# Linear attention and a phase mixer on one core: two batches' k and v in runs of nine tokens, their product in quarters of the array, and a new order of issue

## The chip, the cores and the metric

The kernel runs on one core of one Trainium2 chip. The metric is the device time of one execution in microseconds (us), as the median over several executions.

The engines are TensorE (PE, with its weight loads as PEld), VectorE (DVE), ScalarE (ACT), GpSimd (POOL) and SyncE (SP). Each works through its own queue of instructions in order; they wait for each other through semaphores. Transfers are issued from the queues of SP, ACT and POOL. Those that change the type on the way (fp32 in memory, fp16 on chip) are issued by POOL.

## The reference

Eight batches, eight heads, 576 tokens, head width 64. First a linear attention without softmax, normalised per head, then a mixer over tokens with a phase that comes from the data.

```python
kv  = einsum('bhsd,bhse->bhde', k, v)
out = einsum('bhsd,bhde->bhse', q, kv)
x   = out / sqrt(mean(out * out, -1) + 1e-6) * g_norm      # then (8, 576, 512)
theta = x @ w_theta
y = w_tok_r @ (x * cos(theta)) + w_tok_i @ (x * sin(theta))    # over tokens
u = x + y
result = u + relu(u @ w_ch)
```

## The kernel before

The kernel is a list of small tasks. Each has an engine and a function that issues its instructions. `TURNS`, a list of task numbers written out by hand, gives the one order in which the tasks are issued, and so the order of each engine's queue; a letter behind a number says which engine takes a task that several could do (A for ACT, D for DVE), and `r16` or `r4` stands for that many matmuls on constants, which keep TensorE busy while it has nothing else.

A batch's 576 tokens are four tiles of 128 (j = 0 to 3) and a tail of 64 (j = 4), whose eight heads are packed in halves on 128 partitions. Per batch:

- `load k`, `load v`, `load q`: fp32 k and v through SP, two buffers each (`NKV`); q through POOL as fp16, three buffers.
- `kv`: the product of k and v for each pair of heads (`kv_piece`), and `ko`: its copies into a block diagonal tile `kbd` (`kv_out`).
- `qt` and `qo`: q is turned by TensorE against the identity and copied from PSUM, in batches below `QD`; from batch `QD` on a DMA transpose does it, issued by SP (`qd`, `q_turn_dma`).
- `raw`: turned q times `kbd`. `sq`, `ss`, `rt`, `x`: squares (ACT), their sums (DVE), the power -1/2 (POOL), and the scaled x (DVE), which reads `raw` in PSUM.
- `xt` and `xo`: x turned and copied. `th`: the matmul with `w_theta`. `pt`, `ar`, `ab`, `si`, `co`: reduction of the angle, sine and cosine. `z`: x times both. `zv`: the tail's z, moved by four small transfers issued by POOL.
- `y`: the mix over tokens, for two halves of the columns (y0, y1) and four groups of channels, each in three thirds of three matmuls; the last third needs all z and the moved tail. `um`: u.
- `ut`, `uo`, `v`, `fin`, `st`: u turned back, its matmul with `w_ch`, the sum with relu, the store.

Once, at the beginning, the two token matrices are turned (`wt`, copied by `wo`), and `w_ch` is scaled (`wc`). SP's queue holds back batch 1's k and v until the imaginary token matrix has landed (`hold s`). PSUM has two banks for turned tiles, two for `raw` and four for everything else (`acc`); batch 0's `raw` tiles are in those four as well.

The layout of k and v in SBUF matters here. From batch 1 on, a partition holds four tokens in a row of each head (1024 bytes), and a second transfer brings the last 64 tokens to 64 partitions of a fifth slice (256 bytes each), whose other 64 partitions hold zeros (`pad`). The product then takes five matmuls over 128 rows for each head. In batch 0 a head's 576 tokens lie as nine tokens on each of 64 partitions (2304 bytes in one run), two heads of a pair above each other on 128 partitions:

```python
    def pairs_in(eng, dst, src, b, lo, hi):
        eng.dma_start(
            out=nines(dst)[:, lo:hi, :],
            in_=src[b].rearrange("h (p j) d -> (h p) (j d)", j=NN).rearrange(
                "(n r) x -> r n x", r=P)[:, lo:hi, :],
        )
```

and the product takes nine matmuls over 64 rows for each head, even heads in one quarter of the array, odd heads in the opposite quarter. SP loads k of batch 0 in two transfers, ACT loads v in two.

Of the kernel before, what the change touches and what calls it, by code (L numbers as in the profile page):

```python
# [29 lines left out]
0 2 8 1 4 9 3 5 6 7 11 12 13 r16 29 14 30 15 37 44 45A 38A 32 31D 33 39 46 40 51 34 41 52 47 42 35D  # L30
48 36A 58 65 53 66 54 59 49 67 10 43 55 60 61 68 56 50 62 69 70 16 r4 129 57 125 17 130 63 126 72 18
73D 121 19 71 81 122A 74 20 22 82D 64 21 108 133 109D 198 99 134A 83 199 100D 200 90 75 84 91D 85
127 101 137 76 86 128D 87 92 88 93 102 77 138 131 123 110 132D 94 89 78 111 79 96 205 95 103 112 80
113 206 207 97 114 124 98 115 208 116 159 210A 209D 160 211 212D 232 139 119 118 120 117 140 233D
213 225 214 104 226D 135 155 215 227 228 105 106 216 163 156 218 164 136D 28D 229 230 219D 217 231
220 221 255 234 222 23 24 201 197 26A 107 223 202 157 161 256 246 141 224 158 162 239 165 257 203
240 235 142 247D 204 357 248 166 236 258 249 143 241 259 358 237 260 250 167 168 151 152 147 144 148
145 242 252 353 388 366 514 377 251 238 243 244 25 146 264 265D 245 149 169 273 261 253 262 170 274D
266 153 282 150 154 27D 267 283 275 181 284 276 360 254 268 285 361 286 362 363 191 287 182 288 269
277 289 270 290 263 364D 278 293 291 292 359 294 271 192 365 186 183 188 389 184 187 390 185 279 525  # L40
# [3 lines left out]
403 404D 322 436 384 437 175 502 503 504 304 305 396 385 438 306 397 342 405 386 343 398 327 400 406  # L44
376 399 508 509 347 510 387 407 408 401 328 348 511 193 409 421 329 412 344 512 410 413 194 422 513D
# [5 lines left out]
579D 675 561 447 544 448 449 558 676 667 559 450 574 545 575 495 580 581 582 546 490 668 562 492 455  # L51
# [5 lines left out]
599 604 605 600 707 730 614 718D 731 601 816 619 620 732 817 733 606 826 709D 602 818 734 695 719  # L57
720 847 827 621 615 848 828 697 721 622 722 628 616 617 710 723 711 698 829 618 735 736 819 849 712
713 820 952 724 850 714 851 830 737 738 629 715 953 954 955 643 833 625 630 623 956 834 957 624 644
759 739 716 725 831 835 836 626 740 741 760 838 865 959 839 837 866D 852 631 499 627 945 632 500  # L60
# [5 lines left out]
1097D 873 1098 788 995 996 789 985 778 899 1100 986 900 1111 887 776 647 1121 1101 987D 1102 1112  # L66
777 1103 779 901 888 1022 895 889 780 785 790 896 1004 890 902 1113 1104 988 897 989 990 898 1114
903 904 905 997 891 991 906 1005D 1115 1023 992 998 892 791 1024 893 993 792 1025 999 1000 894 1026
# [753 lines left out]
```

## Time and profile before

| | |
|---|---|
| median of 3 runs | 225.78 us (225.51 to 227.9) |
| profiled execution: time, span | 224.09 us, 222.3 us |
| busy: PE, PEld | 202.9 us (91%), 143.2 us (64%) |
| busy: DVE, ACT, POOL | 175.2 us (79%), 131.6 us (59%), 103.4 us (47%) |
| mean granted clock of TensorE | 0.977 |
| transfers | 40.88 MB, mean 184 GB/s |

How to read it: the span runs from the first to the last instruction of the profiled execution; its time includes what lies around that. A row of a timeline or a chain begins with start and length in us. A row of a group ends in busy time, mean length of one, and idle time before it with the releaser behind an arrow. A matmul's length covers its way through the array, so matmuls in a row overlap, and the time that each adds is the stretch divided by their number. A row of transfer issues has their number, their size, and the median time from issue to landing.

### The profile page before, as it was taken

How to read it: one execution, taken by the hardware profiler on the slowest of the kernel's cores; microseconds unless marked ns; L12 is line 12 of the kernel's file. 1: busy time of each engine (PE TensorE's matmuls, PEld its weight loads, DVE VectorE, ACT ScalarE, POOL GpSimd, SP SyncE). 2: the span in 40 equal slices, each digit the busy share in tenths (PEclk: the TensorE clock that was granted, in tenths of full speed). 3: DMA queues.
4: the chain of work that ended last, by engine and by line, in shares of the span. 5: the costliest groups of instructions: out<-in, count | busy, mean ns of one | idle time of the engine just before them, and what ended most of it. 6: DMA issues, size and time to landing. Idle time of an engine off the chain costs nothing.

```text
span 222.3 us, 5652 instructions
## 1 busy us (share of the span) xinstructions
PE 202.9 (91%) x2266; PEld 143.2 (64%) x2266; DVE 175.2 (79%) x358; ACT 131.6 (59%) x258; POOL 103.4 (47%) x112
## 2 busy tenths in 40 slices
PE   7397896958999999899999999999999999999992
PEld 2295555634777776676685777776676766676760
DVE  4028677849898798978999899799989889978552
ACT  2036257534685369765999559778564978565041
POOL 8208601599448376536765439380926034212000
PEclk9969799987999999999999999999999999999999
DMA  6999999998969999958999999399734004204324
GB/s 213 243 210 195 252 256 363 282 216 97 169 115 136 232 359 300 202 131 232 289 167 198 218 346 167 93 266 227 209 98 146 0 12 133 86 21 128 111 69 170
DMA packets 58731, 40.88 MB, mean 184 GB/s; under 512 B 28114, under 2 KB 52306, under 8 KB 58706
## 3 DMA queue, kind: packets, MB, share of 16 engines
q1 hardware_dynamic: 43474, 31.73, 55.6%
q0 software_dynamic: 14688, 7.62, 25.1%
q10 hardware_dynamic: 544, 1.18, 1.6%
q8 instruction: 18, 0.29, 0.5%
q14 instruction: 7, 0.06, 0.1%
HBM read 33.06 MB, written 9.44 MB: 191 GB/s over the span
## 4 chain that ended last, share of the span: by engine, by line
PE 64%; DMA 24%; POOL 4%; issue 2%; SPq 2%; DVE 2%; ACT 0%; POOLq 0%; DVEq 0%
PE y L516 30%; DMA vt<-in_v_dram 11%; PE v L435 9%; PE th L435 9%; DMA wn<-in_moe_w_tok_i_dram 7%; PE kv L279 5%; PE xps L296 3%; PE ups L296 3%; PE raw L338 2%; DMA zt<-zf 2%; DMA qe<-in_q_dram 2%; DMA out_dram<-ot 2%; PE th L438 2%; POOL rt L376 2%; SPq L194 1%
## 5 line engine op out<-in xcount | busy, mean ns | idle before, releaser
L376 POOL TENSOR_TENSOR rt<-ss,mhalf 128x8 f32<-128x8 f32 (+1 forms) x40 | 62.1, 1556 | 60.2 <-DVE ss L369 56.7
L516 PE MATMUL y<-wT,zm 128*128 128x320 f16 (+1 forms) x512 | 77.9, 287 | 0.7 <-DVE zm L493 0.7
L516 PEld LDWEIGHTS <-zm 128*128 128x128 f16 x512 | 47.8, 98 | 15.2 <-DVE zm L493 0.9
L521 DVE SCALAR_TENSOR_TENSOR wn<-y,gcol,xT 128x320 f16<-128x320 f32 (+1 forms) x64 | 32.0, 511 | 8.9 <-PE y L516 8.6
L435 PE MATMUL th<-wth,xT 128*128 128x512 f16 x128 | 33.6, 390 | 0.0
L451 ACT ACTIVATE pt<-th 128x512 f32<-128x512 f32 (+1 forms) x40 | 22.0, 553 | 17.5 <-PE th L435 16.2
L435 PE MATMUL v<-wch,wn 128*128 128x512 f16 x128 | 32.1, 379 | 0.0
L499 POOL DMA_DIRECT2D zt<-zf x32 | 17.6, 557 | 30.5 <-DVE zf L493 17.0
L480 ACT ACTIVATE sc<-arg,quarter 128x512 f16<-128x512 f32 (+1 forms) x40 | 26.8, 675 | 3.8 <-DVE arg L465 3.8
L542 ACT ACTIVATE us<-ups 128x512 f32<-128x512 f16 (+1 forms) x40 | 21.6, 551 | 12.3 <-PE ups L296 11.0
L556 DVE SCALAR_TENSOR_TENSOR ot<-v,us 128x512 f32<-128x512 f32 (+1 forms) x40 | 25.0, 632 | 4.3 <-ACT us L542 1.8
L457 DVE SCALAR_TENSOR_TENSOR arg<-pt,th 128x512 f32<-128x512 f32 (+1 forms) x40 | 24.8, 628 | 2.2 <-ACT pt L451 1.7
L473 ACT ACTIVATE sc<-arg 128x512 f16<-128x512 f32 (+1 forms) x40 | 23.1, 586 | 5.1 <-DVE arg L457 5.1
L369 DVE TENSOR_REDUCE ss<-sqb 128x8 f32<-128x520 f32 x32 | 22.0, 687 | 4.2 <-ACT sqb L360 4.1
L360 ACT ACTIVATE sqb<-raw 128x512 f32<-128x512 f32 x32 | 19.0, 595 | 10.0 <-PE raw L338 9.6
L399 DVE TENSOR_TENSOR x<-raw,rt 128x512 f16<-128x512 f32 x32 | 21.9, 684 | 3.7 <-POOL rt L376 3.7
L493 DVE TENSOR_TENSOR zm<-x,sc 128x1024 f16<-128x1024 f16 x32 | 21.7, 685 | 2.1 <-ACT sc L480 1.9
L279 PE MATMUL kv<-vt,kt 128*64 128x64 f32 x560 | 18.6, 223 | 3.1 <-DMA vt<-in_v_dram 3.1
L251 ACT ACTIVATE xT<-xps,gcol 128x512 f16<-128x512 f16 (+1 forms) x24 | 15.1, 632 | 10.1 <-PE xps L296 10.0
L279 PEld LDWEIGHTS kv<-vt,kt 128*64 128x64 f32 x560 | 17.5, 138 | 4.3 <-issue 1.9
L516 PE MATMUL y<-wT,zt 128*128 128x320 f16 (+1 forms) x64 | 18.8, 294 | 0.6 <-DMA zt<-zf 0.6
L435 PEld LDWEIGHTS <-xT 128*128 128x128 f16 x128 | 12.0, 101 | 10.2 <-issue 1.4
(73 smaller groups left out, 237.1 us busy)
## 6 DMA issues: line engine op xcount, KB each, us to landing
out_dram<-ot SPq DMA_DIRECT2D x32, 256.0 KB, 3.0
kt<-in_k_dram SPq DMA_DIRECT2D x7, 1024.0 KB, 7.5
vt<-in_v_dram SPq DMA_DIRECT2D x7, 1024.0 KB, 10.9
qh<-in_q_dram POOLq DMA_DIRECT2D x7, 512.0 KB, 10.2
kt<-in_k_dram SPq DMA_DIRECT2D x2, 576.0 KB, 4.8
vt<-in_v_dram ACTq DMA_DIRECT2D x2, 576.0 KB, 9.4
zm<-in_moe_w_ch_dram SPq DMA_DIRECT2D x1, 1024.0 KB, 11.5
zt<-zf POOLq DMA_DIRECT2D x32, 32.0 KB, 3.6
```

The costliest lines, as they stand in the source:

```text
L279: nc.tensor.matmul(t[i * D:(i + 1) * D, hp - lo, :], kt[b % NKV][:, 2 * hp + i, j, :], vt[b % NKV][:, 2 * hp + i, j, :], start=(j == 0), s ...
L369: nc.vector.reduce_sum(out=ss[:], in_=sq_sb.pop((b, j))[:], axis=AXX)
L376: nc.gpsimd.tensor_tensor(out=rt[:], in0=ss[:], in1=mhalf[:, 0:h], op=ALU.pow)
L399: nc.vector.tensor_tensor(out=x_pair[b, p][:, :, a * HC:(a + 1) * HC].rearrange("p t (h e) -> p h t e", e=D), in0=r[:].rearrange("p (h t e ...
L435: nc.tensor.matmul(t[:], lhs[:, kc, columns(j)], w[:, kc, :], start=first, stop=last)
L451: nc.scalar.activation(out=pt[:], in_=th_ps[b, j][:], func=AFT.Copy, bias=MAGIC)
L457: nc.vector.scalar_tensor_tensor(out=arg[:, 0, :], in0=pt_sb.pop((b, j))[:], scalar=MAGIC, in1=th_ps.pop((b, j))[:], op0=ALU.subtract, op1 ...
L473: nc.scalar.activation(out=sc[:, 0, :], in_=arg_sb[b, j][:, 0, :], func=AFT.Sin, bias=0.0, scale=-TURN * SHRINK,)
L480: nc.scalar.activation(out=sc_sb[b, j][:, 1, :], in_=arg_sb.pop((b, j))[:, 1, :], func=AFT.Sin, bias=quarter[:], scale=-TURN * SHRINK,)
L516: nc.tensor.matmul(t[:, 0:hi - lo], s, wT[:, w, lo:hi], start=n == 0, stop=n == len(z) - 1)
L521: nc.vector.scalar_tensor_tensor(out=uTb[b % NUT][:, c, lo:hi], in0=y_ps.pop((b, h, c))[:, 0:hi - lo], scalar=gcol[:, 0:1], in1=xTb[b % NX ...
L556: nc.vector.scalar_tensor_tensor(out=ot[:], in0=v_ps.pop((b, j))[:], scalar=0.0, in1=u_sb.pop((b, j))[:], op0=ALU.max, op1=ALU.add,)
```

## The change

1. The k and v of batches 0 and 1 (`NINES = 2`) are loaded in nine-token runs. A transfer now brings several heads side by side to 64 partitions: for batch 0 two heads each, four transfers on SP (k and v of heads 0 to 3) and four on ACT (k and v of heads 4 to 7); for batch 1 four heads each, four transfers on SP. Batch 1 no longer loads tails.
2. `kv_quad` replaces `kv_piece` for these batches. It goes round the four quarters of the array: partitions 0 to 63 and 64 to 127 as rows, and two halves of the columns. The two row halves write to two PSUM banks, so the copies are twice as many and half as wide.
3. `QD` goes from 2 to 3: batch 2's q is turned on TensorE (16 + 2 transposes, five copies), and three DMA transposes go.
4. The zero fill for batch 3's tails moves from DVE at the start to POOL, beside that for batch 2.
5. `TURNS` is new throughout. At the start: q of tiles 2 and 0 is turned ahead of the first product; the real token matrix is loaded behind the first `rt` on POOL and no longer ahead of it; there are five more matmuls on constants. Later: the products of batches 2 and 3 are issued earlier relative to the token mix of batches 0 and 1, and the first mix of batch 0 finishes its four y1 groups ahead of the first `th` of batch 1.

```diff
-    QD = 2
+    QD = 3
     NKV = 2
+    NINES = 2
...
-    def pairs_in(eng, dst, src, b, lo, hi):
+    def pairs_in(eng, dst, src, b, r, lo, n, at):
         eng.dma_start(
-            out=nines(dst)[:, lo:hi, :],
-            in_=src[b].rearrange("h (p j) d -> (h p) (j d)", j=NN).rearrange(
-                "(n r) x -> r n x", r=P)[:, lo:hi, :],
+            out=nines(dst)[r * D:(r + 1) * D, at:at + n, :],
+            in_=src[b, lo:lo + n].rearrange("h (p j) d -> p h (j d)", j=NN),
         )
...
+    def kv_quad(b, g, los, n, k_):
+        if k_ == 0:
+            for lo in los:
+                kv_ps[b, lo] = ps.tile([P, n, D], FP32, tag="acc", bufs=4, name="kv")
+        for j in range(NN):
+            for s in range(2):
+                for r in range(2):
+                    rows, js = slice(r * D, (r + 1) * D), slice(j * D, (j + 1) * D)
+                    nc.tensor.matmul(
+                        kv_ps[b, los[r]][s * D:(s + 1) * D, k_, :],
+                        nines(kt[b])[rows, 2 * g + s, js], nines(vt[b])[rows, 2 * g + s, js],
+                        start=(j == 0), stop=(j == NN - 1),
+                    )
...
-    for a, (lo, hi) in enumerate(((0, NH2), (NH2, NHP))):
-        both = [add(f"load {x}0{'ab'[a]}", e, lambda e=eng, t=t, src=src, lo=lo, hi=hi: pairs_in(e, t[0], src, 0, lo, hi))
-                for x, e, eng, t, src in (("k", "SP", nc.sync, kt, k), ("v", "ACT", nc.scalar, vt, v))]
+    for a, e, eng in ((0, "SP", nc.sync), (1, "ACT", nc.scalar)):
+        both = [add(f"load {x}0{'ab'[a]}{r}", e, lambda eng=eng, t=t, src=src, a=a, r=r: pairs_in(eng, t[0], src, 0, r, 4 * a + 2 * r, 2, 2 * a))
+                for x, t, src in (("k", kt, k), ("v", vt, v)) for r in range(2)]
...
+        if b < NINES:
+            k_ = [add(f"load {x}{b}n{r}", "SP", lambda t=t, src=src, r=r: pairs_in(nc.sync, t[b], src, b, r, HH * r, HH, 0), old)
+                  for x, t, src in (("k", kt, k), ("v", vt, v)) for r in range(2)]
...
-        pad(nc.vector, 1)
```

The order of the first tasks on two queues, by name (batch and tile or part behind it):

```
TensorE before: idle16, kv 0 0, kv 0 1, qt 0 0, qt 0 2, kv 0 2, raw 0 0, raw 0 2, qt 0 1, kv 0 3, qt 0 3, qte 0 4, raw 0 1, rawe 0 4, raw 0 3, idle4, wt 4, wt 2, xt 0 0, wt 0, xt 0 1, th 0 0, xte 0 4, wt 6, xt 0 3, th 0 1, xt 0 2, wt 3, th 0 3, wte 8, th 0 2, wt 5, wt 1, the 0 4, kv 1 0 to 1 3
TensorE after:  idle16, qt 0 2, qt 0 0, kq 0 0, qt 0 1, qt 0 3, raw 0 2, idle4, qte 0 4, kq 0 1, raw 0 0, raw 0 1, rawe 0 4, raw 0 3, idle5, wt 4, wt 2, xt 0 0, xt 0 1, th 0 0, xt 0 3, th 0 1, wte 8, xte 0 4, th 0 3, xt 0 2, wt 6, wt 0, th 0 2, wt 5, the 0 4, wt 1, wt 3, kq 1 0, kq 1 1
POOL before:    q0 (4 loads), wth, toki, tokie, tokr, tokre, rt 0 0, rt 0 2, rt 0 1, rte 0 4, rt 0 3, q1, zv 0 (4), rt 1 0, rt 1 1, q1e (2), pad
POOL after:     q0 (4 loads), wth, toki, tokie, rt 0 2, tokr, tokre, rt 0 0, rt 0 1, rt 0 3, rte 0 4, q1, zv 0 (4), pad 1, rt 1 0, rt 1 1, q1e0, pad 0, q1e1
```

More of the change, by code (lines that the diff above doesn't have):

```diff
@@ L35 @@
[L35 to L39, printed above, removed]
@@ L653 @@
         ko = {}
-        for lo, n in ((0, 2), (2, 2)) if b == 0 else ((0, NHP),):
+        banks = (((0, 1), 1), ((2, 3), 1)) if b == 0 else (((0, 2), 2),) if b < NINES else (((0,), NHP),)
+        for los, n in banks:
             first = prev = None
-            for hp in range(lo, lo + n):
-                t = add(f"kv {b} {hp}", "PE", lambda b=b, hp=hp, lo=lo, n=n: kv_piece(b, hp, lo, n),
-                        [*k_got[b, hp], prev], [] if prev else [PS_ACC])
-                first, prev = first or t, t
-            outs = [add(f"ko{n} {b} {i}", "DVE" if i and b < QD else "ACT",
+            if b < NINES:
+                for k_ in range(n):
+                    g = los[0] // 2 + k_
+                    t = add(f"kq {b} {g}", "PE", lambda b=b, g=g, los=los, n=n, k_=k_: kv_quad(b, g, los, n, k_),
+                            [*k_got[b, 2 * g], prev], [] if prev else [PS_ACC, PS_ACC])
+                    first, prev = first or t, t
+            else:
+                for hp in range(NHP):
+                    t = add(f"kv {b} {hp}", "PE", lambda b=b, hp=hp: kv_piece(b, hp, 0, NHP),
+                            [*k_got[b, hp], prev], [] if prev else [PS_ACC])
+                    first, prev = first or t, t
+            outs = [add(f"ko{n} {b} {i}{lo}", "DVE" if i and b < QD else "ACT",
                         lambda e, b=b, i=i, lo=lo, n=n: kv_out(b, i, lo, n, e),
-                        [prev, *of("raw", b - 2)], alt=("ACT", "DVE")) for i in range(2)]
+                        [prev, *of("raw", b - 2)], alt=("ACT", "DVE")) for lo in los for i in range(2)]
             first.readers = outs
-            last["kv", b] = prev
-            for hp in range(lo, lo + n):
-                ko[hp // 2] = outs
-        ko[2] = ko[0] + ko[1]
+            last["kv", b, los[0]] = prev
+            for lo in los:
+                for hp in range(lo, lo + n):
+                    ko.setdefault(hp // 2, []).extend(x for x in outs if x not in ko.get(hp // 2, []))
+        ko[2] = ko[0] + [x for x in ko[1] if x not in ko[0]]
         turned_by = {}
```

73 lines of the change are left out of this document (36 added, 37 removed), and 57 rows, old and new, of the table TURNS.

## The prediction

> **What bounds the kernel now.** I read the page first, then the busy time by stage, the chain that ended last, and the timeline of the first 55 us. From the page:
>
> ```profile
> span 222.3 us, 5652 instructions
> PE 202.9 (91%) x2266; PEld 143.2 (64%) x2266; DVE 175.2 (79%) x358; ACT 131.6 (59%) x258; POOL 103.4 (47%) x112
> PE 64%; DMA 24%; POOL 4%; issue 2%; SPq 2%; DVE 2%; ACT 0%; POOLq 0%; DVEq 0%
> ```
>
> TensorE is the busy engine, yet a quarter of the chain is transfers. The busy time by stage says where (columns: stretch in us; its length; busy time and instructions of PE, PEld, DVE, ACT, POOL; granted clock; DMA share; GB/s):
>
> ```profile
> 21.00:34.00 13.00, 11.84 (x91) 7.15 (x88) 9.72 (x22) 5.89 (x11) 4.83 (x4) 0.87 1.06 245
> 34.00:38.90 4.90, 2.88 (x82) 2.66 (x83) 3.75 (x8) 3.58 (x9) 0.62 (x2) 1.00 1.09 370
> 52.20:80.00 27.80, 27.75 (x310) 20.26 (x308) 24.37 (x52) 16.61 (x35) 16.58 (x18) 1.00 1.15 178
> 80.00:213.20 133.20, 131.66 (x1454) 93.64 (x1452) 117.27 (x232) 91.35 (x179) 60.59 (x60) 1.00 0.72 167
> ```
>
> From 52.2 to 213.2 TensorE stands still for 0.05 + 1.54 = 1.6 us of 161. Whatever reaches that stretch is bought or sold at TensorE's own price, and nothing else counts there unless it makes a new wait. Before 52.2 the engine waits much (2 us in the 4.9 from 34.0 alone), and in the 13 us before those its clock is 0.87. The chain shows for what:
>
> ```profile
> 5.09 15.70 DMA wn<-in_moe_w_tok_i_dram
> ...
> 24.03 12.54 DMA vt<-in_v_dram
> ...
> 46.81 4.10 DMA qe<-in_q_dram
> ...
> 52.21 1.80 PE th L435 x8
> ...
> 54.59 2.89 PE y L516 x24
> 57.48 0.22 PE xps L296 x4
> ...
> 81.18 11.70 DMA vt<-in_v_dram
> ```
>
> The load of the imaginary token matrix ends at 20.8; it holds back k and v of batch 1, whose last piece lands at 36.6; only then can the product of batch 1 finish, at a point that I call E (38.8, from the timeline below). The first theta of batch 1 starts at 52.2. So two stretches decide: up to E, and from E to 52.2.
>
> **Stretch one, up to E.** The timeline of before:
>
> ```profile
> 13.10 1.04 PE L296 MATMUL qps<-ident,qh 128*128 128x128 f16 x8
> 13.22 0.53 POOL L223 DMA_DIRECT2D wnt<-in_moe_w_tok_r_dram  x1 [6.43 <-DMA qh<-in_q_dram]
> 14.06 1.54 PE L272 MATMUL kv<-vt,kt 64*64 64x64 f32 x36
> 15.54 0.62 PE L338 MATMUL raw<-kbd,qT 128*128 128x128 f16 x8
> 17.45 4.89 POOL L376 TENSOR_TENSOR rt<-ss,mhalf 128x8 f32<-128x8 f32 x3 [3.69 <-DVE ss L369]
> 18.30 0.54 ACT L301 CAST kbd<-kv 64x128 f16<-64x128 f32 x2 [0.76 <-DVE kbd L303]
> 27.58 1.41 PE L435 MATMUL th<-wth,xT 128*128 128x512 f16 x4
> 33.30 0.63 PE L438 MATMUL th<-wth,xT 128*64 128x256 f16 x8
> 36.71 2.09 PE L279 MATMUL kv<-vt,kt 128*64 128x64 f32 x64 [1.78 <-DMA vt<-in_v_dram]
> ```
>
> ```profile
> kt<-in_k_dram SPq DMA_DIRECT2D x2, 576.0 KB, 4.8
> vt<-in_v_dram ACTq DMA_DIRECT2D x2, 576.0 KB, 9.4
> kt<-in_k_dram SPq DMA_DIRECT2D x7, 1024.0 KB, 7.5
> kt<-in_k_dram SPq DMA_DIRECT2D x7, 128.0 KB, 7.5
> out_dram<-ot SPq DMA_DIRECT2D x32, 256.0 KB, 3.0
> out_dram<-ot SPq DMA_DIRECT2D x16, 64.0 KB, 3.4
> wn<-in_moe_w_tok_r_dram POOLq DMA_DIRECT2D x1, 576.0 KB, 17.7
> wnt<-in_moe_w_tok_r_dram POOLq DMA_DIRECT2D x1, 72.0 KB, 11.2
> ```
>
> SP now fetches k and v of heads 0 to 3, ACT those of heads 4 to 7. SP's share used to land first (4.8 us against 9.4), so the first group is whole by about 7 us instead of 10. That buys nothing, because the new order puts the turning of q ahead of the first product on TensorE, and q lands at about 13.1 whoever loads k and v: POOL's waiting load was released at 13.22, and the same bytes share the engines. So: turns 13.10 + 1.04, then 36 products (the cold row, 1.54), which before had run during the wait for q. The copies of the product into its block diagonal are four casts of 64x128 before and eight of 64x64 now, six of them in a row on ACT; at 0.54 / 2 = 0.27 us each (the nearest row; a cast half as long may cost less) 1.6 us. First raw at 13.10 + 1.04 + 1.54 + 1.6 = 17.3 against 15.54: 1.7 late.
>
> The lateness grows behind it. The second group's casts stand on DVE behind the first x, which waits for its power on POOL; the real token matrix's two load issues (0.53 us by the row of the tail, each) stand on POOL between the first power and the second, and a power is 4.89 / 3 = 1.63. I get the first power at 19.1 to 20.7, the next three from about 23 on, and the first turning of x at 27.0. The second theta then starts at about 29.1, where before it was 27.58. The rest of batch 0's thetas took 33.93 - 27.58 = 6.35; two more token turns now stand in front (5 transposes each, 0.3 us): end at 29.1 + 7.0 = 36.1. Before they ended at 33.93, and the product of batch 1, begun behind them, waited 1.78 us for v and ended at E = 36.71 + 2.09 = 38.8. That wait is the cover; it is used up now.
>
> The product of batch 1 has 72 matmuls of 64 rows for 80 of 128. In four quarters they could take half the time; but 36 in 1.54 on two quarters (cold) and 64 in 2.09 on full rows are 43 and 33 ns each, so the spacing hardly depends on the form. I take 33 ns, 2.4 us (bounds: 1.2 and 3.1, from half that and from 43 ns). E = 36.1 + 2.4 = 38.5 against 38.8: **-0.3** (bounds -3, if products run at half and the copies cost half, to +4, if loads come late, below). The pads of the product's unused rows move from DVE to POOL, where they stand between the moves of z and the first power of batch 1, behind a product that ends 4 us before that power can start: nothing; without that cover 1 us.
>
> **Stretch two, E to the first theta of batch 1.**
>
> ```profile
> 46.21 0.69 DVE L399 TENSOR_TENSOR x<-raw,rt 128x512 f16<-128x512 f32 x1 [0.92 <-POOL rt L376]
> 47.42 0.68 DVE L493 TENSOR_TENSOR zm<-x,sc 128x1024 f16<-128x1024 f16 x1
> 52.17 0.47 DVE L253 TENSOR_SCALAR xT<-xps,gcol 128x512 f16<-128x512 f16 x1
> ```
>
> Product, casts, raw, square, sum, power, x: that chain ran 46.90 - 38.8 = 8.1 us and is unchanged. Batch 0's last z, which all last thirds of the token mix await, came 1.2 us behind it; now a copy of x's transpose (0.47) and its turning stand before it on DVE, 2.1 us behind: E + 10.2. Then 4 thirds of three matmuls and two more, at 2.89 / 24 = 0.12 each, 2.2 us: first theta at E + 12.4 against 13.4, **-1.0**. By then two more thirds are done (12 + 2 against 9 + 3), **-0.7**, and the turn of q's tails, which awaited its load until 50.9, stands behind this work and not before it. Bounds: -2.5, and +1.5 if q of batch 1, issued some 3 us later behind the powers, is late.
>
> **The rest.** Batch 2's queries: 18 transposes at 0.22 / 4 us on a full TensorE, **+1.0**. Their five copies lie on ACT and DVE, which are busy 59% and 79% of the span: nothing, or up to 1 if they hold back a power. Three DMA transposes go from SP:
>
> ```profile
> L324 SPq DMA_TRANSPOSE qD<-qh x4: 1232/1242/1296, 58.2 to 67.0; - x4
> ```
>
> At 1.24 us of issue each that frees 3.7 us of SP, and the loads for batches 3 and 4 stand ahead of more stores. That can remove the wait behind the 81.18 row, and with it at most the 1.54 us that PE idles after 80; but batch 3's product is now issued ahead of batch 1's token mix, so its load is needed at about 65, and can cost as much. I take 0, between -1.5 and +1.5. The end is alike: a last store on a buffer of three, 0.
>
> **Sum:** -0.3 - 1.0 - 0.7 + 1.0 = -1.0. Span 222.3 to 221.3; the profiled execution's 224.09 to 223.1. It stood 1.7 below the median of the runs, so the forecast there is 225.78 - 1.0 = **224.8**, with its own range 222.5 to 227.5.
>
> **The rivals.**
>
> *Half-wide loads (slower).* k and v of batches 0 and 1 now go to 64 partitions at a time. If such a load runs at half speed, SP's first four take 4.3 us more (an estimate: the 4.8 us to landing, less some 0.5 of start that does not double); ACT's and q follow on the same engines, so q, the token matrix and the hold behind it move by 4.3, and batch 1's loads, doubled too, overrun the products by about another 1. It decides as soon as q lands later than about 15. For it: a 64-partition store of 64 KB lands in 3.4 us, one of 256 KB from 128 partitions in 3.0. Against: the 128 KB tails of k, also 64 partitions, land in the same 7.5 as the 1024 KB ahead of them. Time 224.8 + 5.3 = 230.1. The Trainium skill (SBUF — State Buffer, "Door 1: The DMA port swizzle") says that partitions 0 to 63 reach half of the DMA ports and that two such loads do not add up. By that rule this case happens.
>
> *The real token matrix late (slower).* Its load moves from the start of POOL's queue to behind the first power, about 20.7, into the crowd of batch 1's loads. TensorE wants it right after the second theta, at 30, with batch 0's other thetas queued behind. At the 11.2 us that the tail's load took it lands at 32 to 33, a stall of about 3: 227.8; at 17.7 it would be 8. For it: the queues are full then (DMA share 1.06). Against: it was queued behind four others when it took 17.7.
>
> *Quarters overlap and loads lead (faster).* The two products take half (-0.8, -1.2) and 1.0 of the 1.54 us of idle after 80 goes: 224.8 - 3.0 = 221.8. For it: four quarters have separate rows, columns and banks. Against: the equal spacing above. The Trainium skill (TensorEngine Tiling (Array Packing), "Tiling Modes") has four 64x64 tiles work in parallel, which is this case; no run here shows it yet. That they do not overlap at all is in the forecast already.
>
> **How the numbers follow.** Forecast 0.38, half-wide loads 0.24, late token matrix 0.17, overlap 0.21. A measurement of this kernel can tell about 1% from no change: below 223.5 or above 228.0. Faster: the overlap case, most of it (0.19), and the low edge of the forecast (0.10), 0.29. Slower: half-wide loads (0.23), half of the token case (0.09), the forecast's high edge (0.03), 0.35. Same: 0.36. The range runs from 220.0, below the overlap case, to 231.0, above the half-wide case.
>
> **What would show it.** Right: q lands near 13 and k, v of heads 0 to 3 near 7; the first raw at about 17; E near 38.5; the first theta of batch 1 at about 51; idle of PE after that below 3 us. Wrong: k0 and v0 landing after 9 (half-wide); TensorE waiting at the turns of the real token matrix near 30; products of 64x64 at 20 ns or less; a wait for k or v of batch 3 near 65; q of batch 1 later than 40.

## The result, and the profile after

The changed kernel takes **233.21 us** (231.95 to 234.09) against 226.44 for the kernel before, measured beside it: 1.029 times the time, interval 1.021 to 1.037. The forecast was 224.8, within 1% of before, range 220.0 to 231.0: it was wrong, and the range missed. (Ratios below leave out disturbed runs of both kernels; where a ratio and two medians differ, the ratio decides.)

The profiled execution took 231.95 us. From its page:

```profile
span 230.2 us, 5844 instructions
PE 206.2 (90%) x2353; PEld 144.2 (63%) x2353; DVE 172.8 (75%) x357; ACT 136.3 (59%) x275; POOL 104.0 (45%) x113
PE 56%; DMA 17%; POOL 8%; DVE 8%; ACT 5%; issue 4%; POOLq 0%; DVEq 0%; ACTq 0%
```

TensorE has 3.3 us more work, the span is 7.9 longer. The busy time by stage (columns as in the prediction) shows where the rest lies:

```profile
21.00:34.00 13.00, 9.38 (x50) 5.00 (x51) 7.71 (x18) 5.24 (x12) 8.19 (x8) 0.61 0.90 185
34.00:38.90 4.90, 4.70 (x39) 2.81 (x38) 3.05 (x8) 3.80 (x7) 0.00 (x0) 0.98 1.06 237
52.20:80.00 27.80, 22.93 (x338) 17.18 (x335) 22.24 (x47) 18.15 (x38) 16.72 (x19) 1.00 1.19 233
80.00:220.00 140.00, 138.09 (x1475) 99.46 (x1474) 123.96 (x248) 93.13 (x184) 66.92 (x66) 1.00 0.68 150
```

After 80 us TensorE idles 1.9 us of 140, about as before (1.54 of 133). The idle time is added ahead of that: from 52.2 to 80 it idles 4.9 us where it had idled 0.05, and from 21 to 34 it works 9.4 us where it had worked 11.8, at a granted clock of 0.61 instead of 0.87. The transfers of that stretch bring 185 GB/s instead of 245. From the first theta of batch 1 to the end it takes 171.4 us (58.82 to 230.2), before 170.1 (52.2 to 222.3): 6.6 of the 7.9 us are lost by then. The chain that ended last (start, length):

```profile
1.48 11.54 DMA qh<-in_q_dram
...
25.50 3.29 POOL rt L384 x3
...
30.34 0.96 POOL rt L384
31.30 14.93 DMA qh<-in_q_dram
...
54.84 6.88 DMA qe<-in_q_dram
```

The load of batch 0's queries is followed by batch 0's powers, behind which batch 1's queries are issued; these take 14.9 us, and their tails end the stretch. The k and v of batch 1, on which the forecast had its eye, are not in this chain. The timeline of the changed kernel, the rows that answer to the forecast's steps:

```profile
13.06 1.03 PE L304 MATMUL qps<-ident,qh 128*128 128x128 f16 x8 [5.33 <-DMA qh<-in_q_dram]
14.03 2.20 PE L288 MATMUL kv<-vt,kt 64*64 64x64 f32 x72
16.32 1.35 ACT L309 CAST kbd<-kv 64x64 f16<-64x64 f32 x6 [2.03 <-PE kv L288]
17.03 0.91 PE L346 MATMUL raw<-kbd,qT 128*128 128x128 f16 x4
18.85 1.28 PE L288 MATMUL kv<-vt,kt 64*64 64x64 f32 x72
19.67 1.68 POOL L384 TENSOR_TENSOR rt<-ss,mhalf 128x8 f32<-128x8 f32 x1 [13.44 <-DVE ss L377]
22.82 0.43 ACT L309 CAST kbd<-kv 64x64 f16<-64x64 f32 x2 [3.56 <-DVE kbd L311]
24.48 0.76 PE L346 MATMUL raw<-kbd,qT 128*128 128x128 f16 x4 [4.03 <-DVE kbd L311]
32.86 1.69 PE L443 MATMUL th<-wth,xT 128*128 128x512 f16 x4
39.20 0.63 PE L446 MATMUL th<-wth,xT 128*64 128x256 f16 x8
40.76 2.33 PE L288 MATMUL kv<-vt,kt 64*64 64x64 f32 x144
46.28 0.62 PE L304 MATMUL qps<-ident,qh 128*128 128x128 f16 x8 [2.27 <-DMA qh<-in_q_dram]
58.82 1.03 PE L443 MATMUL th<-wth,xT 128*128 128x512 f16 x4
61.86 0.27 PE L304 MATMUL qps<-ident,qe 128*128 128x128 f16 x2 [2.01 <-DMA qe<-in_q_dram]
```

To 19.67 the forecast holds to half a microsecond. Then the second raw stands 4.03 us for casts, the thetas of batch 0 end at 39.8 and not at 36.1, the product of batch 1 ends at E = 43.1 and not at 38.5, and its first theta starts at 58.8 and not near 51.

### The profile page after: what moved, and what is told of

Its sections match the earlier page's. It is cut to its first block, busy times and chain, and to the rows that moved or that the text cites. A ratio compares the mean times of both kernels' runs of the same rounds, so it can differ in the third digit from the quotient of the medians.

```text
span 230.2 us, 5844 instructions
## 1 busy us (share of the span) xinstructions
PE 206.2 (90%) x2353; PEld 144.2 (63%) x2353; DVE 172.8 (75%) x357; ACT 136.3 (59%) x275; POOL 104.0 (45%) x113
## 4 chain that ended last, share of the span: by engine, by line
PE 56%; DMA 17%; POOL 8%; DVE 8%; ACT 5%; issue 4%; POOLq 0%; DVEq 0%; ACTq 0%
PE y L524 23%; DMA qh<-in_q_dram 14%; PE v L443 9%; PE th L443 7%; POOL rt L384 6%; PE kv L271 4%; DMA qe<-in_q_dram 3%; DVE ss L377 3%; PE ups L304 3%; PE raw L346 2%; PE xps L304 2%; ACT kbd L309 1%; PE qps L304 1%; ACT sqb L368 1%; PE v L446 1%
## 5 line engine op out<-in xcount | busy, mean ns | idle before, releaser
L384 POOL TENSOR_TENSOR rt<-ss,mhalf 128x8 f32<-128x8 f32 (+1 forms) x40 | 63.6, 1593 | 69.1 <-DVE ss L377 69.0
L524 PE MATMUL y<-wT,zm 128*128 128x256 f16 (+1 forms) x512 | 79.0, 290 | 2.2 <-DVE zm L501 1.8
L529 DVE SCALAR_TENSOR_TENSOR wn<-y,gcol,xT 128x256 f16<-128x256 f32 (+1 forms) x64 | 31.5, 510 | 6.2 <-PE y L524 6.1
L507 POOL DMA_DIRECT2D zt<-zf x32 | 17.1, 542 | 37.0 <-DVE zf L501 20.2
L550 ACT ACTIVATE us<-ups 128x512 f32<-128x512 f16 (+1 forms) x40 | 21.9, 555 | 15.6 <-PE ups L304 11.7
L252 ACT ACTIVATE xT<-xps,gcol 128x512 f16<-128x512 f16 (+1 forms) x25 | 16.1, 644 | 5.9 <-PE xps L304 5.7
L443 PEld LDWEIGHTS <-wn 128*128 128x128 f16 x128 | 11.7, 98 | 10.6 <-issue 0.6
L524 PE MATMUL y<-wT,zt 128*128 128x256 f16 (+1 forms) x64 | 18.3, 286 | 0.0
L473 DVE TENSOR_SCALAR arg<-arg 128x512 int32<-128x512 int32 (+1 forms) x40 | 15.7, 398 | 0.5
```

Source lines behind the costliest of these rows:

```text
L384: nc.gpsimd.tensor_tensor(out=rt[:], in0=ss[:], in1=mhalf[:, 0:h], op=ALU.pow)
L443: nc.tensor.matmul(t[:], lhs[:, kc, columns(j)], w[:, kc, :], start=first, stop=last)
L524: nc.tensor.matmul(t[:, 0:hi - lo], s, wT[:, w, lo:hi], start=n == 0, stop=n == len(z) - 1)
L529: nc.vector.scalar_tensor_tensor(out=uTb[b % NUT][:, c, lo:hi], in0=y_ps.pop((b, h, c))[:, 0:hi - lo], scalar=gcol[:, 0:1], in1=xTb[b % NX ...
L550: nc.scalar.activation(out=d[:], in_=tr_ps.pop(("u", b, j))[:].rearrange("p n c -> p (n c)"), func=AFT.Copy, scale=TURN,)
```

## The experiments

The kernel before was measured beside each group of runs: medians 225.73 us (runs 1 to 4), 224.15 (5 to 8), 224.37 (9 to 12), 224.32 (13, 14) and 224.59 (15, 16). Across groups the ratios are compared.

Two theories stood at the start. **L**: the half-wide loads (64 partitions at a time) are slow. **O**: the order of issue is, which makes batch 0's chain late and puts batch 1's queries behind it.

### 1 to 4: the loads alone, the order alone

**Run 1**: the changed kernel, but k and v of both batches come to 128 partitions in each transfer; the quarters stay (the pairs of heads that share a step change, and with them the addresses of the casts).

```diff
-        eng.dma_start(out=nines(dst)[r * D:(r + 1) * D, at:at + n, :], in_=src[b, lo:lo + n]...)
+        if r == 0:
+            eng.dma_start(out=nines(dst)[:, at:at + n, :],
+                          in_=src[b].rearrange("h (p j) d -> (h p) (j d)", j=NN)...[:, at:at + n, :])
```

> The changed kernel in its own issue order, with one edit: each pair of half-wide loads (64 partitions each) of k and v of batches 0 and 1 becomes one load over all 128 partitions, and the quarters of the product take the heads as they then lie. Same bytes, same runs of 2304 bytes, same matmuls and copies. Theory L (half-wide loads are the cause: they ran at about 220 GB/s where the old ones reached 400): k and v of batch 0 all land by 12.5 us, those of batch 1 by 36, batch 1's q by 42 instead of 46.2, and the kernel falls by 3 to 5 us, to 228 to 230. Theory O (the order is the cause: batch 0's chain of powers ends 6 us later, and q of batch 1 is issued behind it at 31.3): the late issue stays, the first theta of batch 1 stays after 56, and the time falls by less than 1.5, to 232 or more.

227.45 us, 1.0135 of before (1.007 to 1.020). Against the changed kernel that is 5.8 us less by the medians and 1.5%, some 3.5 us, by the ratios: beside this group the kernel before was itself faster.

**Run 2**: the changed kernel with one task of POOL's queue moved.

```diff
-rt 0 2, load tokr, load tokre, rt 0 0, rt 0 1, rt 0 3, rte 0 4, load q1
+rt 0 2, load tokr, load tokre, load q1, rt 0 0, rt 0 1, rt 0 3, rte 0 4
```

> The changed kernel with one task moved: POOL issues the load of batch 1's q right behind the real token matrix (about 22.5 us) and no longer behind batch 0's five powers (31.3). Theory O: q lands by about 39, TensorE no longer waits 2.3 us for it at 46.3, and the kernel falls by 2 to 4 us, to 229 to 231. Theory L: the loads share a saturated set of engines, so q early makes k and v of batch 1 as much later (past 42), and the time stays within 1.5 us of 233.

231.67 us, 1.031 (1.025 to 1.037): no gain that can be measured. From this run's timeline:

```profile
14.58 1.03 PE L304 MATMUL qps<-ident,qh 128*128 128x128 f16 x8 [7.82 <-DMA qh<-in_q_dram]
42.24 2.33 PE L288 MATMUL kv<-vt,kt 64*64 64x64 f32 x144
45.32 0.61 PE L304 MATMUL qps<-ident,qh 128*128 128x128 f16 x8
49.88 0.28 PE L346 MATMUL raw<-kbd,qT 128*128 128x128 f16 x2 [1.74 <-issue]
60.28 1.03 PE L443 MATMUL th<-wth,xT 128*128 128x512 f16 x4
```

The queries are issued at 23.93, 7.4 us earlier. They take 18.8 us instead of 14.9, land near 42.7, and TensorE no longer waits for them; it waits 1.74 us at the next raw instead, for a reason that the trace does not show. The product of batch 1 ends at 44.6, 1.5 later than in the changed kernel, but not because of the move: batch 0's queries had landed 1.5 later in this execution (14.58 against 13.06), before the moved load was issued. From E to the first theta it takes 15.7 us in both.

**Run 3**: the other way round. The kernel before, its loads of k and v of batch 0 and the two large ones of batch 1 cut into halves of 64 partitions, nothing else changed.

```diff
-        eng.dma_start(out=nines(dst)[:, lo:hi, :], in_=...[:, lo:hi, :])
+        for c in range(2):
+            at = slice(c * D, (c + 1) * D)
+            eng.dma_start(out=nines(dst)[at, lo:hi, :], in_=...[at, lo:hi, :])
...
+        for at in (slice(0, D), slice(D, P)) if b == 1 else (slice(0, P),):
+            eng.dma_start(out=dst[at, hs, 0:NJ, :], in_=...[at])
```

> The kernel before in its own order, with one edit: the loads of k and v of batch 0, and the two large ones of batch 1, are cut into two of 64 partitions each. Same bytes, same runs, same tasks. Theory L: the last of v of batch 1 lands 3 to 5 us after 36.6, the product of batch 1 ends near 42.5, and the kernel rises to 229 to 231. Theory O: within 1.5 us of before, 226 to 228.

231.19 us, 1.028 (1.019 to 1.038): the changed kernel's loss, without its order. It is not where the expectation had it: the product of batch 1 ends at 39.5, not near 42.5, and TensorE then waits 3.65 us for batch 1's queries (until 44.94).

**Run 4**: the kernel before and its order of tasks, with nine-token runs over 128 partitions and the product in quarters. Batch 2's queries stay with the DMA, and k of batch 0 comes on SP and v on ACT, as before.

```diff
-QD = 3, order of the changed kernel, loads of 64 partitions
+QD = 2, order of the kernel before, loads of 128 partitions; pad 1 behind zv 0 on POOL
```

> The kernel before in its own order, with the new layout and product alone: nine-token runs in batches 0 and 1, loaded over 128 partitions, products in four quarters, the zero fills on POOL; q of batch 2 still by DMA transposes. Theory L: the layout costs nothing once its loads are wide; without batch 1's tail loads v lands 1 us earlier, and the time is 224 to 226.5. Theory O says the same of this one. If the quarters or their doubled copies are a cost of their own, it comes out above 228.

225.88 us, 1.004 (0.998 to 1.011): the same as before. The quarters themselves cost nothing that can be measured. From its timeline:

```profile
33.25 2.48 PE L289 MATMUL kv<-vt,kt 64*64 64x64 f32 x144
49.68 1.02 PE L451 MATMUL th<-wth,xT 128*128 128x512 f16 x4 [0.15 <-DVE wn L537]
```

E is 35.7, three us ahead of the kernel before, and the first theta 2.5 ahead; yet the end is not earlier. Runs 8 and 11 come back to that.

L holds in both directions. By the ratios the half-wide loads cost 1.5% (the changed kernel against run 1) to 2.8% (run 3 against the kernel before), 3.5 to 6.4 us. What the loads do is seen where little else is on the wire: the stretch 27.5 to 30 us (clock, DMA share and GB/s at the end of the row). The changed kernel:

```profile
27.50:30.00 2.50, 2.49 (x16) 1.58 (x15) 1.74 (x4) 1.02 (x2) 2.50 (x2) 0.50 1.05 223
```

Run 1:

```profile
27.50:30.00 2.50, 2.24 (x18) 1.41 (x17) 1.74 (x5) 1.28 (x2) 2.50 (x3) 0.74 1.04 402
```

The kernel before, in one us in which it loads k and v of batch 1 to 128 partitions:

```profile
25.00:26.00 1.00, 1.00 (x4) 0.41 (x3) 1.00 (x2) 0.13 (x1) 1.00 (x2) 0.50 1.04 354
```

The engines are as busy in all three, and move 223 GB/s to 64 partitions where they move 402 to 128 in the same runs of nine tokens. No run cut a load in two at full width; that the width costs and not the number of transfers is read from these rates. With this the Trainium skill (SBUF — State Buffer, "Door 1: The DMA port swizzle") agrees: half the partitions reach half the ports.

### 5, 6 and 13: which of the loads, and through what

**Run 6**: run 1 with batch 1's loads half-wide again. **Run 13**: run 1 with batch 0's half-wide again.

```diff
-        if r == 0:
+        if b == 1:          # run 13: b == 0
+            eng.dma_start(out=nines(dst)[r * D:(r + 1) * D, at:at + n, :], in_=src[b, lo:lo + n]...)
+        elif r == 0:
             eng.dma_start(out=nines(dst)[:, at:at + n, :], ...)
```

> The changed kernel with batch 0's four pairs of loads over 128 partitions and batch 1's four large loads still over 64 partitions each. It tells which of the half-wide loads cost the 5.8 us. If it is batch 0's late chain, the time is near that with all loads wide: 227.5 to 228.5. If it is batch 1's k and v, which landed 30.1 to 39.7 us, the time is near the changed kernel's: 231 to 233.

232.85 us, 1.040 (1.032 to 1.048).

> The changed kernel with batch 1's k and v loaded over 128 partitions and batch 0's left half-wide, the complement of the run in which only batch 1's were half-wide (232.85 us, ratio 1.040). If batch 1's loads alone cost the 5.8 us, this one is near the version with all loads wide: ratio 1.010 to 1.020, 226.5 to 229. If the two share the cost, or either alone is enough, it stays at 1.025 to 1.035.

228.36 us, 1.017 (1.009 to 1.025). So batch 1's loads cost 5.4 us by the medians against run 1 (2.6% by the ratios), batch 0's 0.9 (0.3%). Together that is 6.3 us and 3.0%, where all half-wide loads cost 5.8 us and 1.5% above: comparisons across groups differ by about 1%, so it is shown which loads cost more, but the sizes only roughly. What they cost it through is one row of the chain. In run 1:

```profile
30.41 11.50 DMA qh<-in_q_dram
```

In run 6:

```profile
30.42 15.76 DMA qh<-in_q_dram
```

In run 13:

```profile
31.58 11.53 DMA qh<-in_q_dram
```

In run 3, the order of before with half-wide loads:

```profile
28.43 16.47 DMA qh<-in_q_dram
```

The load of batch 1's queries, itself unchanged and full-wide, is issued at the same time in runs 1 and 6 and takes 4.3 us longer where k and v of batch 1 stand half-wide ahead of it. In the kernel before, its issue at 25.18 us to landing (the last column of the transfers of that microsecond):

```profile
qh<-in_q_dram POOLq DMA_DIRECT2D x1, 512.0 KB, 11.2
```

TensorE's timeline in run 6:

```profile
38.62 2.32 PE L294 MATMUL kv<-vt,kt 64*64 64x64 f32 x142 [0.18 <-DMA vt<-in_v_dram]
46.23 0.92 PE L317 MATMUL qps<-ident,qh 128*128 128x128 f16 x8 [4.36 <-DMA qh<-in_q_dram]
60.86 1.03 PE L456 MATMUL th<-wth,xT 128*128 128x512 f16 x4
```

and in run 1:

```profile
37.98 2.33 PE L289 MATMUL kv<-vt,kt 64*64 64x64 f32 x144
41.96 0.62 PE L312 MATMUL qps<-ident,qh 128*128 128x128 f16 x8 [0.73 <-DMA qh<-in_q_dram]
55.90 1.14 PE L451 MATMUL th<-wth,xT 128*128 128x512 f16 x4
```

The half-wide k and v themselves are waited for 0.18 us. E differs by 0.6, the wait for the queries by 3.6, the first theta by 5.0, the whole by 5.4. The price of a slow load is paid by the transfer behind it.

In the changed kernel itself the second theta of batch 1 starts 5.0 us later than in run 1 (62.52 against 57.54). Of these 2.8 are lost up to E, and 2.0 in the wait for the tails (the row at 61.86). Of the 2.8, 1.1 are lost by batch 0's first theta (30.75 against 29.65), and 1.7 come of its first two thetas, which took 1.89 and 1.69 us at a granted clock of 0.55; in run 1 they took 1.04 and 1.03 at 1.00. That clock does not follow the loads: run 14 below, with full-wide loads and the same as run 1 up to there, had 1.89 and 1.73 us at 0.53, and run 16, with half-wide loads, 1.04 twice at 1.00.

**Run 5**: run 1 with the move of run 2.

> The changed kernel with the loads of k and v of batches 0 and 1 over all 128 partitions (as in the run before that measured 227.45 us) and, in addition, the load of batch 1's queries put on POOL right behind the real token matrix, some 8 us earlier. If the 1.7 us that are left above the kernel before come from the order of the loads (batch 1's queries issued at 30.41 instead of 25.18 us), the queries land near 37 instead of 41.92 us and the time falls to 225.5 to 226.5. If they come from batch 2's queries on TensorE or from the rest of the issue order, it stays at 227 to 228.

228.7 us, 1.022 (1.015 to 1.029): no gain, and above both expectations. TensorE waits 2.09 us at the raw behind the queries instead. With full-wide loads the queries are no longer what comes last.

### 9, 10, 14, 15, 16: what is left

With full-wide loads the changed kernel still stands 1 to 2% above the kernel before. Three more single suspects were tried, beside the queries of run 5.

**Runs 9 and 10**: the four tasks that cast batch 0's second group (two casts each) ahead of `x 0 2`, in the changed kernel and in run 1.

```diff
-x 0 2, qoe 0 4, qo 0 3, ko1 0 13, ko1 0 03, sq 0 0, ko1 0 02, ko1 0 12, ss 0 0
+qoe 0 4, qo 0 3, ko1 0 13, ko1 0 03, ko1 0 02, ko1 0 12, x 0 2, sq 0 0, ss 0 0
```

> The changed kernel with one thing changed in its issue order: the four casts of the second half of batch 0's product into the block-diagonal tile stand ahead of the scaling of third 2 (x 0 2) and of the square of third 0 on DVE and ACT, not behind them. In the changed kernel VectorE came to these casts only after x 0 2, which waits for a power on POOL, and TensorE stood 4.03 us for them before its second raw. If this stall sets when batch 1's product ends, the stall falls to about 2 and the end of that product moves up by 1.5 to 2.5 us; by the theory that batch 1's queries, which land late behind half-wide loads, come last, the total falls by less than 1 us, to 232 to 233; by the theory that batch 0's chain comes last, to 230.5 to 231.5.

231.55 us, 1.032 (1.027 to 1.037): no gain on the changed kernel's 1.029.

> The same move of the four casts, with k and v of batches 0 and 1 loaded over 128 partitions (measured without the move at 227.45 us, TensorE idle 4.03 us before its second raw, the end of batch 1's product at 40.3 us against 35.7 with the same loads in the order of the kernel before). The stall should fall to about 1 us. If the issue order of batch 0 is what is left above the kernel before, the end of batch 1's product moves to 37 to 38 and the time to 225.5 to 226.5. If batch 1's queries or batch 2's set it, the time stays at 227 to 228.

227.57 us, 1.013 (1.008 to 1.019). The stall did go, as run 10's timeline shows:

```profile
21.16 0.54 PE L354 MATMUL raw<-kbd,qT 128*128 128x128 f16 x4 [1.46 <-DVE kbd L319]
27.69 1.89 PE L451 MATMUL th<-wth,xT 128*128 128x512 f16 x4 [0.36 <-DVE xT L255]
37.58 2.33 PE L289 MATMUL kv<-vt,kt 64*64 64x64 f32 x144
```

The wait fell from 4.03 to 1.46, and the second raw came 2.4 earlier than in run 1; the product of batch 1 came 0.4 earlier and the end not at all. The first theta was still 2.0 earlier (27.69 against 29.65); then the first two thetas took 1.89 and 1.57 us at a granted clock of 0.56, which lost 1.6 of it again. Against run 14, where the clock was as low, E came 2.2 earlier (39.9 against 42.1) and the first theta of batch 1 1.5 (55.6 against 57.2). So the move does gain at E, and the clock took most of it back.

**Run 14**: run 1 with batch 2's queries turned by DMA again.

```diff
-    QD = 3
+    QD = 2
 SP:  ..., load v3, load v3e, load k4, ...
+     qde 2 2, qd 2 0, qd 2 1 between load v3e and load k4
```

> The changed kernel's order with all loads wide (227.45 us, ratio 1.0135) and batch 2's queries turned by DMA as in the kernel before, the three issues behind the load of batch 3's v on SP's queue. If the turns on TensorE are what is left of the loss, the 18 transposes and their waits go and the ratio falls to 0.995 to 1.005. If the issue order is what is left, it stays at 1.010 to 1.020; the turns by DMA may also hold back the loads of batch 4 behind them on SP, which would show as a wait for k or v and a ratio above 1.02.

228.65 us, 1.018 (1.010 to 1.026): nothing regained. From the first theta of batch 1 to the end it takes 169.9 us, in run 1 169.7: in this order the turns are not what is left.

**Runs 15 and 16**: batch 0's last z ahead of batch 1's squares and sums, in run 1 and in the changed kernel.

```diff
-sq 1 0 (ACT), ab 0 3, ss 1 0 (DVE), sq 1 1, wc 3, si 0 3, qo 1 2, wc 1, co 0 3, ..., x 1 1, xo 1 1, ss 1 2, z 0 3
+ab 0 3, si 0 3, co 0 3, sq 1 0, z 0 3, ss 1 0, sq 1 1, wc 3, qo 1 2, wc 1, ..., x 1 1, xo 1 1, ss 1 2
```

> The changed kernel with all loads wide (227.45 us, ratio 1.0135) and the sine, cosine and product of batch 0's last third (si 0 3, co 0 3, z 0 3, with ab 0 3 ahead of them) put before batch 1's first square and sum. In the kernel before z 0 3 starts 8.6 us after the end of batch 1's product, here 11.3. If that step is what is left of the order's loss, z starts near 45, the wait of 1.78 us goes, the first theta of batch 1 comes 1.5 to 2 us earlier and the ratio falls to 1.003 to 1.009. If the thirds of batch 1 (delayed 1.3 us on ACT) come last instead, the ratio stays at 1.010 to 1.020.

227.31 us, 1.012 (1.006 to 1.017).

> The same move in the changed kernel with its half-wide loads. TensorE waits there 1.78 us for the same product and later 2.01 us for batch 1's last queries, which land at 61.7 us. If the z chain ends last, the time falls by 1.5 to 2 us (ratio 1.020 to 1.025); if the queries do, the gain is swallowed by the wait for them: within 0.7 us of the changed kernel (ratio 1.027 to 1.034).

234.02 us, 1.040 (1.033 to 1.046), above both expectations. In run 15 z starts at 45.55, 5.75 earlier than in run 1 (51.30), and TensorE waits for x instead:

```profile
49.44 0.38 PE L354 MATMUL raw<-kbd,qT 128*128 128x128 f16 x4 [2.06 <-DVE x L415]
55.57 1.03 PE L451 MATMUL th<-wth,xT 128*128 128x512 f16 x4
```

The first theta does not move (55.6 against 55.9). What is left of the order's loss is not in any one of these steps; it stays open what would have to move together.

Where it lies can be read from the traces. In every run with the changed order, from the first theta of batch 1 to the end takes 169.3 to 171.4 us, in the kernel before 170.1. In run 1 that theta starts 3.7 us later than before (55.9 against 52.2): 1.5 are lost up to E (40.3 against 38.8), and 2.2 from there on. The last thirds of the token mix took 3.9 us (52.04 to 55.90) at a granted clock of 0.59; in the changed kernel they took 2.3 (56.52 to 58.82) at 1.00.

### 7, 8, 11, 12: what the quarters are worth in the other order

All four start from run 4. **Run 8** moves `load q1` with its tails behind `load tokre` on POOL. **Run 11** adds two moves on SP:

```diff
 POOL
-tokr, tokre, rt 0 0, rt 0 2, rt 0 1, rte 0 4, rt 0 3, load q1, ..., load q1e0, load q1e1
+tokr, tokre, load q1, load q1e0, load q1e1, rt 0 0, rt 0 2, rt 0 1, rte 0 4, rt 0 3
 SP (run 11)
-load k3, qde 2 2, qd 2 0, qd 3 0, qd 2 1, st 0 20, qd 3 1, load k3e, load v3, st 0 30, load v3e, st 0 10, load k4, st 0 00, load k4e, load v4, load v4e
+load k3, load k3e, load v3, load v3e, qde 2 2, qd 2 0, qd 3 0, qd 2 1, st 0 20, qd 3 1, load k4, load k4e, load v4, load v4e, st 0 30, st 0 10, st 0 00
```

> The same kernel without batch 2's queries on TensorE (measured at 225.88 us), with the three loads of batch 1's queries moved on POOL right behind the real token matrix. If the three us won at the end of batch 1's product are given back because the first raws of batch 1 wait for their queries, the time falls by 0.5 to 1.5 us, to 224.5 to 225.5, and the load of q lands before 36. If they are given back at 80 to 100 us in the wait for batch 4's v, nothing changes: 225.5 to 226.5.

223.82 us, 0.991 (0.985 to 0.996): 1.3% below run 4, more than either expectation had. Its trace still has the wait of 1.5 us for v between 80 and 110 us that is shown below for run 4; where it gained is not shown.

> A version meant to beat both: the order of the kernel before, full-width loads and quarters, batch 1's queries right behind the real token matrix (measured at 223.82 us, 0.991 of before), and on SP's queue the loads of batch 3's k and v directly behind the first of them, those of batch 4 ahead of the stores of batch 0's output. The wait of 1.5 us for batch 4's v near 92 us should go, and with it 1 to 1.5 us of the total: 222.3 to 223.3, ratio 0.983 to 0.988. If the loads then collide with batch 2's and 3's queries, which come through POOL's queue, the wait only moves: 223.5 to 224.5.

221.60 us, **0.987** (0.983 to 0.992): it beats both kernels. Its interval overlaps run 8's, so what the two moves on SP add is shown by the trace and not by the time. Part of the lead that run 4 had lost is seen in the stretch 80 to 100 us. The kernel before:

```profile
80.00:100.00 20.00, 19.02 (x282) 13.68 (x281) 17.78 (x34) 15.65 (x31) 11.84 (x13) 1.00 1.05 236
```

Run 4:

```profile
80.00:100.00 20.00, 18.02 (x263) 13.59 (x262) 15.00 (x29) 14.33 (x28) 9.72 (x11) 0.91 0.99 190
```

Run 11:

```profile
80.00:100.00 20.00, 20.00 (x299) 14.48 (x297) 18.95 (x35) 16.18 (x33) 12.43 (x12) 1.00 0.83 189
```

Run 4's longest wait of TensorE in that stretch (us in total, times, longest):

```profile
PE kv L272 <- DMA vt<-in_v_dram: 1.5, 1, 1.5
```

A load of v that stood behind stores and transposes on SP's queue stopped an engine that had come early; with the loads ahead of them TensorE has no idle time there. From the first theta of batch 1 to the end run 4 takes 173.8 us and run 11 169.8; the 2.0 us of idle time are half of that.

**Runs 7 and 12** add batch 2's queries on TensorE to run 4 and to run 11, with the turns placed by hand.

```diff
-    QD = 2
+    QD = 3
-qde 2 2, qd 2 0, qd 2 1 (SP)
+qte 2 4 before v 0 2; qt 2 0, qt 2 2 before ut 0 1; qt 2 1 before raw 2 0; qt 2 3 before y0 1 2 0 (TensorE)
+qd 3 0 behind raw 2 1, qd 3 1 behind raw 2 2 (SP)
```

> The kernel with the loads order and issue order of before, k and v in nine-token runs loaded over 128 partitions and the product in quarters (measured alone at 225.88 us), and in addition batch 2's queries turned on TensorE instead of by DMA, their turns issued a few steps ahead of each raw. 18 transposes more cost some 1.0 us of TensorE; the transposing DMA issues of batch 2 leave SP's queue, in which one of them held the loads behind it for 16.1 us. If the turns only cost, 226.5 to 227.5. If the earlier loads of batches 3 and 4 also spare the wait for v at 88 us (1.5 us) and the thinner work behind it, 224.5 to 225.5.

234.2 us, 1.033 (1.022 to 1.044): a miss of both expectations. TensorE waited 4.1 us ahead of one product and 2.4 for the v of another.

> The kernel of the run above it, with batch 2's queries turned on TensorE as well, and the DMA turns of batch 3's queries behind the loads of batches 3 and 4 on SP's queue. In the run with batch 2's queries on TensorE that measured 234.2 us the queue of loads stood still at 60 to 70 us (53 GB/s), because the turns of batch 3 stood ahead of the loads. If that was the cause of its 8 us, this one is within 1 us of the run above it: 222.5 to 224.5. If the 18 turns themselves, with their evictions on ACT and VectorE, are what costs, it stays 4 us or more above: 227 or more.

225.65 us, 1.0045 (1.001 to 1.008): between its two expectations. With the loads ahead most of run 7's loss is gone, but run 12 stays some 1.7% above run 11. The stretch 60 to 70 us in run 11:

```profile
60.00:70.00 10.00, 9.96 (x152) 7.36 (x147) 8.99 (x20) 7.21 (x16) 6.28 (x10) 1.00 1.11 141
```

And in run 12:

```profile
60.00:70.00 10.00, 8.30 (x104) 5.63 (x100) 7.06 (x17) 5.87 (x12) 6.12 (x9) 1.00 0.53 80
```

TensorE loses 1.7 us there, 1.2 of it in waits for the copies that have to follow each turn, beside the turns' own time. This is a price in this placing, not the least that the turns could cost.

## Why the prediction was wrong, point by point

- **The rival "half-wide loads" held, and it was not made the likeliest.** Its time, 230.1, was within 3.1 of the result, and its price of 5.3 lies within what the runs give (3.5 to 6.4 us by the ratios, 5.5 to 5.8 by the medians). The step that failed is the first of stretch one: the half-wide loads were taken at full rate, where the runs show 223 GB/s against 402. The forecast did so on the strength of the 128 KB tails, which land with the load ahead of them and so say nothing of a rate. Of the 2.9% that the kernel lost, the loads are 1.5 by run 1, and the rest of the change, forecast at -1.0 us, is the other 1.35.
- **Its place and its deciding point were wrong.** It was to decide "as soon as q lands later than about 15". q landed at 13.06, and the price came all the same. The sign given beside it did show: v of heads 0 to 3, issued on SP from 2.23 us on, took 8.5 and 10.4 us to land, where "near 7" was forecast; the wait for q hid it. The price was paid through batch 1 (runs 6 and 13), and there not by k and v but by the queries behind them.
- **"+1.5 if q of batch 1 is late" was mis-sized.** The issue was 6.1 us later (31.30 against 25.18) and not 3, and the load took 14.9 us and not 11.2: it landed near 46 instead of 36.4. TensorE waited 2.27 us for it and 2.01 more for its tails.
- **The zero fills were not all free.** The one that moved cost nothing, as forecast. The other, for batch 2's tails, stood on POOL between the two loads of the tails, from 53.91 to the issue at 54.84, in the chain that ended last: 0.9 us that is in no term of the forecast. No run takes it away alone.
- **Up to the first power the sum was right**: 13.06, 17.03, 19.67 against 13.1, 17.3, 19.1 to 20.7. Two errors cancel in it. A matmul on fp32 operands leaves two records in the trace, so "36 in 1.54" were 18, and "80 of 128 rows" were 40; the 36 products took 2.20 us. On the other side the casts took 0.22 each and not 0.27, and the first raw began 0.8 us behind the product, while casts were still running.
- **So the spacing of the products was wrong, and the rival "overlap" right in its mechanism.** The row of the kernel before:

```profile
16.31 1.26 PE L272 MATMUL kv<-vt,kt 64*64 64x64 f32 x36
```

  18 matmuls on two quarters took 1.26 us, 36 on four took 1.28 (the row at 18.85), both at a granted clock of 1.00: four quarters work twice as fast. The Trainium skill (TensorEngine Tiling (Array Packing), "Tiling Modes") has four 64x64 tiles work in parallel, and the trace agrees. It changes little for batch 1, where 40 matmuls over 128 rows gave way to 72: 2.33 us, forecast 2.4. That this term came out right is luck: its 33 ns were the spacing of records of matmuls over full rows, two to a matmul, and a matmul in a quarter happened to take about as long as one such record.
- **The second group's casts were seen, but not their chain.** The eight casts of this group into one tile follow each other across two engines in the order of issue (the row at 22.82 waits 3.56 on ACT for VectorE's), so the second raw came at 24.5. Batch 0's thetas ended 3.7 late, at a clock of 0.61. Run 10, with most of this stall gone, ends no earlier; a low clock took back most of what it had gained.
- **-1.0 and -0.7 of stretch two did not come.** From E to the first theta of batch 1 it took 15.7 us, not 12.4. Of that 2.3 are the wait for the queries, and without it z still ended at E + 11.1 and not at E + 10.2. In run 1, with its loads mended, it took 15.6 (from 40.3 to 55.9), the same by chance: the wait for the queries was 0.7 and z ended at E + 10.9 without it, but the last thirds took 3.9 us at the low clock, forecast 2.2. Without the loads' price the order stands at 1.0135 of before, where the forecast had -1.0 us. That batch 1's chain and batch 0's last z wait on each other in turn is shown by run 15; that no better placing of the two exists is not.
- **The rival "late token matrix" did not happen**: TensorE has no wait at its turns; the tail's load took 6.4 us from its issue at 21.90, and not 11.2.
- **"The rest" at 0 was right for the changed kernel**: TensorE idles 1.9 us after 80, as much as before. The wait for batch 3's load near 65 did not come. That the queues' order is worth up to 1.5 us there was seen in the forecast (the 1.54 of idle); run 11 has no idle time left between 80 and 100 us, where the kernel before has 0.98.
- **The +1.0 for batch 2's turns** could not be told from 0 in the changed order (run 14), and was 4 us in the other (run 12 against run 11, placing included).

## What to carry to other kernels

Price a transfer by the partitions it reaches before its bytes, and look for who pays among the transfers behind it on the same engines, not at the tile that it loads. A step that is mended moves the end only if the next wait is mended too: three stalls of 1.8 to 4 us were taken away here one at a time, wholly or for the most part, and none moved the time. What a shorter wait gives can also go again in a lower clock (run 10). A lead at the front of a pipelined kernel can be lost where the loads of later batches come too late to meet it, as in run 4.

## What the hardware showed that was not expected

- Loads to 64 partitions ran at 223 GB/s with the DMA engines as busy as at 402 GB/s to 128. A busy share of 1 tells nothing of the rate.
- The casting load of batch 1's queries, full-wide itself, took 15.8 us behind half-wide traffic and 11.5 behind full-wide traffic.
- Four 64x64 quarters took 36 fp32 matmuls in the time that two took 18 (1.28 against 1.26 us, both at a granted clock of 1.00).
- Batch 0's first two thetas, issued in the same order, took 1.04 and 1.03 us at a granted clock of 1.00 in run 1, and 1.89 and 1.73 at 0.53 in run 14. A difference of 1 to 2 us between two single traces can be no more than this.
